# Output tiles in fp16, cast to fp32 by the software DMA queue, with more buffers and right halves stored between whole rows

## The chip, the cores and the metric

The kernel runs on one core of one Trainium2 chip. The metric is device time in microseconds (us), the median of several executions. All runs in this document are with one core in use. Ratios and their 95% intervals are over fast runs of the same rounds; they are not quite the ratio of the medians quoted beside them. The span of a profile is about 2 us shorter than the device time of the same execution (182.8 and 184.6 us for the kernel before). In the profile's lines PE is the matrix engine, DVE the vector engine, ACT the scalar engine, POOL is GpSimd and SP the sync engine. "DMA engine" means one of the core's 16 DMA engines. A run of bytes is a contiguous piece that a transfer reads or writes, 1 KB or 2 KB here.

## The reference, cut to what matters

Windowed attention (8 batches, 8 heads, 576 positions, head size 64) feeds a soft mixture of experts. Only the end of the second part matters here:

```python
# x: [4608, 512], the attention output; phi: [512, 32]; w1: [8, 512, 1024]; w2: [8, 1024, 512]
...
for e in range(E):
    h = np.maximum(slot_input[e] @ w1[e], 0.0)
    slot_out[e] = h @ w2[e]
slot_out = slot_out.reshape(n_slots, D)          # [32, 512]
c = softmax(logits, axis=1)                      # [4608, 32]; cut
return (c @ slot_out).astype(np.float32)         # [4608, 512] fp32: 9.44 MB
```

All inputs and the output are fp32 in HBM. A row of the output holds 512 numbers: 2 KB in fp32.

## The kernel before: the parts that the argument touches

The loads are issued by GpSimd on the software DMA queue and cast from fp32 to fp16 on the way. The weights `w2` of experts 6 and 7 are loaded by column halves, so that the left half of the output can start while the weights of the right half still arrive. The output then goes out in 26 transfers: 8 left halves of 256 rows each, 10 whole pairs of 128-row blocks, 8 right halves. In the code `fp` is the product in PSUM and `rrow` holds the reciprocals of the softmax row sums.

```python
out_pool = tc.alloc_tile_pool(name="outp", bufs=NSPLIT // 2)      # NSPLIT = 16, NH = 256
...
def combine(half, pair):                       # 256 rows, half of the columns: runs of 1 KB
    ...                                        # two matmuls into PSUM tile fp
    ot = out_pool.tile([128, 2, NH], FP32, name=f"ot{half}_{pair}", tag="ot")
    if pair % 2 == 0:
        ...                                    # ACT: two activations with scale=rrow
    else:
        nc.vector.tensor_tensor(out=ot, in0=fp, in1=rrow[...], op=ALU.mult)
    nc.sync.dma_start(out=out[r0 : r0 + 256, NH * half : NH * half + NH].rearrange("(k p) n -> p k n", k=2), in_=ot)

def combine_full(pair):                        # 256 whole rows: runs of 2 KB
    ot = out_pool.tile([128, 2, DMODEL], FP32, name=f"of_{pair}", tag="of", bufs=5)
    for k in range(2):
        ...                                    # one matmul; ACT scales k = 0, DVE k = 1
    nc.sync.dma_start(out=out[r0 : r0 + 256, :].rearrange("(k p) n -> p k n", k=2), in_=ot)

slot_out(0, ORDER[:6]); slot_out(1, ORDER[:6]); slot_out(0, HALVED)
for pair in range(NSPLIT // 2):
    combine(0, pair)                           # left halves
    ...                                        # expert 6 of the right half after pair 5
slot_out(1, HALVED[1:])
for pair in range(NSPLIT // 2, NFIN // 2):
    combine_full(pair)                         # whole rows
for pair in range(NSPLIT // 2):
    combine(1, pair)                           # right halves
```

The softmax here doesn't subtract the row's maximum and nothing guards it: scores larger than these inputs give would overflow.

## Time and profile before

| | before |
|---|---|
| median of 3 runs | 184.9 us (184.83 to 185.29) |
| busy share of PE, DVE, ACT, GpSimd | 78%, 57%, 49%, 34% |
| last weight landed | 156.95 us |
| last output landed | 181.66 us |
| end of the span | 182.8 us |

The profile's page of the kernel before: the DMA row gives the busy tenths of the 16 DMA engines in 40 slices of the span, the row below it the GB/s that they wrote (a cast load counts with its fp16 side), and the queue rows packets, MB and share.

```profile
span 182.8 us, 5535 instructions
...
DMA  5999999999999999999999999999999999999996
GB/s 88 195 198 211 203 208 206 211 209 204 213 207 204 213 208 204 213 208 204 213 208 204 212 212 213 216 214 214 215 214 216 196 196 183 328 376 387 380 351 219
...
q0 software_dynamic: 24640, 31.10, 97.6%
q1 hardware_dynamic: 7360, 9.56, 14.9%
...
out_dram<-of SPq DMA_DIRECT2D x10, 512.0 KB, 5.5
...
out_dram<-ot SPq DMA_DIRECT2D x16, 256.0 KB, 3.9
```

The DMA engines are full in all but the first and the last slice. Up to slice 34 (about 155 us) they load; about 210 GB/s of fp16 are 420 GB/s of fp32 read. In the last six slices they store. The outputs are nearly all of q1's 9.56 MB.

The end of the chain that ended last, of the kernel before: start, length, engine or DMA, what.

```profile
146.53 10.42 DMA w<-in_moe_w_dram
156.99 0.32 PE so L681 x4
157.33 0.38 ACT so_sb L689
...
162.03 10.45 DMA out_dram<-of x2
172.47 0.68 DVE ot L713
```

It waits for the last weight, and then for transfers of the output. Engines compute only in the gaps.

The waits of the kernel before from 145 us on: who waited for what, us in total, times, longest.

```profile
ACT of L732 <- DMA out_dram<-of: 5.1, 5, 2.7
DVE of L736 <- DMA out_dram<-of: 3.6, 4, 2.0
```

With five buffers for whole-row tiles, ACT and DVE stand still for 8.7 us (the sum of both) until stores free a buffer.

The stretches view of the kernel before, one for whole rows (2 KB runs) and one for right halves (1 KB runs): busy us of PE, weight loads, DVE, ACT and GpSimd, then the granted clock, the DMA share and GB/s.

```profile
165.00:171.00 6.00, 4.07 (x16) 1.92 (x15) 3.85 (x6) 4.10 (x8) 0.00 (x0) 0.64 1.04 384
176.00:180.00 4.00, 0.00 (x0) 0.00 (x0) 0.00 (x0) 0.00 (x0) 0.00 (x0) 0.50 1.03 345
```

Divided over 16 engines, 384 GB/s is one 2 KB run per 85.3 ns, and 345 GB/s one 1 KB run per 47.5 ns. A straight line through these two rates has 37.8 ns for each KB and a fixed part of 9.7 ns for each run. The share of 1.03 says that packets hardly overlap.

### The profile page before, as it was taken

The numbers are of one execution on the slowest core, as the hardware profiler recorded it, in microseconds if no ns is written. First come the engines' busy times: TensorE is split into PE (matmuls) and PEld (weight loads), VectorE is DVE, ScalarE is ACT, GpSimd is POOL, SyncE is SP. The second block draws the span as 40 slices with busy tenths as digits, with TensorE's granted clock in tenths as the row PEclk, the third lists the DMA queues.
The fourth block names the chain that finished last, engine by engine and source line by source line (L and its number), as shares of the span: only waits on it lengthen the run. The fifth ranks groups of instructions, "written<-read, shape, count | busy, mean of one in ns | idle before, by whom it ended". The sixth has DMA issues, their size and how long they took to land.

```text
span 182.8 us, 5535 instructions
## 1 busy us (share of the span) xinstructions
PE 142.9 (78%) x2448; PEld 85.6 (47%) x2448; DVE 104.2 (57%) x225; ACT 90.1 (49%) x161; POOL 62.6 (34%) x86
## 2 busy tenths in 40 slices
PE   0467989999999999999999999998694087746600
PEld 0134556557557557557557557573532063312300
DVE  2585797958767867867867865360502004555700
ACT  2044267667666766766766766734002005644800
POOL 7643644652651751751822935311110110000000
PEclk9999999999999999999999999985569667897555
DMA  5999999999999999999999999999999999999996
GB/s 88 195 198 211 203 208 206 211 209 204 213 207 204 213 208 204 213 208 204 213 208 204 212 212 213 216 214 214 215 214 216 196 196 183 328 376 387 380 351 219
DMA packets 32024, 41.01 MB, mean 224 GB/s; under 512 B 2144, under 2 KB 19680, under 8 KB 32000
## 3 DMA queue, kind: packets, MB, share of 16 engines
q0 software_dynamic: 24640, 31.10, 97.6%
q1 hardware_dynamic: 7360, 9.56, 14.9%
q8 instruction: 19, 0.31, 0.6%
q14 instruction: 5, 0.04, 0.1%
HBM read 62.18 MB, written 9.44 MB: 392 GB/s over the span
## 4 chain that ended last, share of the span: by engine, by line
DMA 48%; PE 27%; issue 7%; ACT 6%; POOL 4%; DVE 3%; SPq 0%; POOLq 0%
DMA w<-in_moe_w_dram 34%; DMA raw<-in_q_dram 8%; DMA out_dram<-of 6%; PE lg L413 5%; PE o_p L344 5%; PE sa L287 4%; ACT p L298 4%; PE sa L276 3%; PE sb L276 3%; ACT of L732 2%; PE u L455 2%; PE rd L394 1%; PE vb L188 1%; PE va L188 1%; POOL w L220 1%
## 5 line engine op out<-in xcount | busy, mean ns | idle before, releaser
L298 ACT ACTIVATE p<-sa 128x960 f16<-128x960 f32 (+2 forms) x24 | 21.4, 890 | 30.2 <-PE sb L287 29.5
L344 PEld LDWEIGHTS <-p 128*128 128x128 f16 (+2 forms) x544 | 19.5, 98 | 12.6 <-issue 8.6
L241 DVE STREAM_TRANSPOSE qk<-raw 128x576 uint32<-128x576 uint32 x16 | 20.0, 1250 | 6.8 <-DMA raw<-in_q_dram 5.9
L250 DVE STREAM_TRANSPOSE qk<-raw 128x320 uint32<-128x320 uint32 (+1 forms) x32 | 21.5, 678 | 0.3
L298 ACT ACTIVATE p<-sb 128x960 f16<-128x960 f32 (+2 forms) x24 | 21.2, 885 | 0.0
L276 PE MATMUL sa<-masks,ident 128*128 128x480 f16 (+2 forms) x48 | 13.8, 372 | 6.6 <-DMA ident<-ident_d 4.9
L413 PE MATMUL lg<-xTd,phi 128*128 128x288 f16 x32 | 18.3, 659 | 0.0
L287 PE MATMUL sa<-qk 32*128 32x160 f16 (+4 forms) x416 | 15.7, 212 | 2.4 <-DVE qk L241 2.4
L287 PEld LDWEIGHTS <-qk 32*128 32x128 f16 x832 | 11.9, 96 | 11.8 <-issue 8.2
L276 PEld LDWEIGHTS <-ident 128*128 128x128 f16 x96 | 8.9, 102 | 17.4 <-issue 8.7
L216 POOL COPY v<-v 32x1024 f16<-32x1024 f16 x8 | 8.3, 1034 | 25.4 <-DVE v L209 22.9
L344 PE MATMUL o_p<-v,p 128*128 128x65 f16 (+1 forms) x288 | 16.4, 201 | 0.7 <-ACT v L197 0.7
L287 PE MATMUL sb<-qk 32*128 32x160 f16 (+4 forms) x416 | 15.7, 212 | 0.0
L232 POOL DMA_DIRECT2D w<-in_moe_w_dram x8 | 5.9, 742 | 27.2 <-DMA w<-in_moe_w_dram 22.8
L366 DVE TENSOR_TENSOR xp<-o_p,rc_p 128x448 f16<-128x448 f32 (+1 forms) x24 | 14.5, 602 | 0.8
L366 DVE TENSOR_TENSOR xd<-o_d,rc_d 128x448 f16<-128x448 f32 (+1 forms) x24 | 14.5, 602 | 0.8
L713 DVE TENSOR_TENSOR ot<-f,rrow 128x512 f32<-128x512 f32 x8 | 5.5, 690 | 15.8 <-PE f L697 15.6
L276 PE MATMUL sb<-masks,ident 128*128 128x480 f16 (+2 forms) x48 | 14.0, 372 | 0.4 <-issue 0.2
L681 PE MATMUL so<-w,hTm 128*32 128x256 f16 x128 | 7.0, 354 | 8.5 <-DMA w<-in_moe_w_dram 7.7
L220 POOL DMA_DIRECT2D w<-in_moe_w_dram x16 | 11.4, 715 | 5.5 <-DMA raw<-in_k_dram 2.1
L188 PE MATMUL va<-vs,orders 32*128 32x256 f16 (+1 forms) x96 | 12.1, 289 | 1.0 <-ACT p L298 1.0
L417 ACT ACTIVATE ET<-lg 128x288 f16<-128x288 f32 x16 | 6.6, 410 | 12.0 <-PE lg L413 11.8
(84 smaller groups left out, 251.7 us busy)
## 6 DMA issues: line engine op xcount, KB each, us to landing
w<-in_moe_w_dram POOLq DMA_DIRECT2D x16, 512.0 KB, 16.6
w<-in_moe_w_dram POOLq DMA_DIRECT2D x6, 1024.0 KB, 28.1
out_dram<-of SPq DMA_DIRECT2D x10, 512.0 KB, 5.5
vs<-in_v_dram POOLq DMA_DIRECT2D x8, 512.0 KB, 13.1
out_dram<-ot SPq DMA_DIRECT2D x16, 256.0 KB, 3.9
raw<-in_q_dram POOLq DMA_DIRECT2D x7, 576.0 KB, 15.1
raw<-in_k_dram POOLq DMA_DIRECT2D x7, 576.0 KB, 15.4
w<-in_moe_w_dram POOLq DMA_DIRECT2D x8, 256.0 KB, 23.3
```

Of the source, the lines that this page charges most:

```text
L188: nc.tensor.matmul(o.rearrange("p (h d) -> p h d", h=4), l, st[:, 0:4, D * r : D * r + D], start=(r == 0), stop=(r == DIL - 1), skip_group ...
L216: nc.gpsimd.tensor_copy(out=vL[b % NV][0:32, :, :, 0:D], in_=vD[b % NV][96:128, :, :, 0:D])
L220: nc.gpsimd.dma_start(out=w1t[e][:, 2 * i : 2 * i + 2, :], in_=src[:, 2 * i : 2 * i + 2, :])
L241: nc.vector.transpose(out=dst, in_=src)
L250: nc.vector.transpose(out=o, in_=i)
L276: nc.tensor.matmul(sps[h // 2][:, h % 2, 0:n], ident, bias[g], start=True, stop=False, skip_group_check=True,)
L287: nc.tensor.matmul(sps[h // 2][:, h % 2, c0 : c0 + w], kt_[32 * h : 32 * h + 32, k0 : k0 + 128, tt], qt_[32 * h : 32 * h + 32, q0 : q0 + w ...
L298: nc.scalar.activation(out=pt, in_=sps[ab][:, :, 0:n], func=AF.Exp, scale=SCALE)
L344: nc.tensor.matmul(o[p0 : p0 + np_, n, :], l, rr, start=(k == 0), stop=(k == len(jobs) - 1), skip_group_check=True,)
L366: nc.vector.tensor_tensor(out=x.rearrange("p t (h d) -> p (t h) d", h=4)[0:nq, u0:u1, :], in0=o[0:nq, 0:n, 0:D], in1=rc[0:nq, 0:n, None].b ...
L413: nc.tensor.matmul(lp, phi4[:, kc].rearrange("p c s -> p (c s)"), rhs, start=(kc == 0), stop=(kc == 3))
L681: nc.tensor.matmul(so[half][32 * a : 32 * a + 32, :], hTm[2 * g + c // 4][:, c % 4, 32 * j : 32 * j + 32], w2t[e][:, c, NH * half : NH * h ...
```

## The change

The intent: half the bytes read from SBUF per output, room for 24 buffers for the 26 output tiles in place of 13 (the last two whole-row tiles reuse buffers), no waits for buffers, and a smoother mix of small and large stores. A cast in flight is done by the software queue only, as the Trainium skill has it ("DMA: Bandwidth & Descriptors", section "SWDGE vs HWDGE vs iDMA"), so the stores move from the sync engine's queue to GpSimd's.

```diff
-    out_pool = tc.alloc_tile_pool(name="outp", bufs=NSPLIT // 2)
+    out_pool = tc.alloc_tile_pool(name="outp", bufs=1)
...
-        ot = out_pool.tile([128, 2, NH], FP32, name=f"ot{half}_{pair}", tag="ot")
+        ot = out_pool.tile([128, 2, NH], FP16, name=f"ot{half}_{pair}", tag=f"ot{half}", bufs=NSPLIT // 2)
...
-        nc.sync.dma_start(
+        nc.gpsimd.dma_start(                      # in combine and in combine_full
...
-        ot = out_pool.tile([128, 2, DMODEL], FP32, name=f"of_{pair}", tag="of", bufs=5)
+        ot = out_pool.tile([128, 2, DMODEL], FP16, name=f"of_{pair}", tag="of", bufs=8)
...
             combine_full(pair)
-        for pair in range(NSPLIT // 2):
-            combine(1, pair)
+            if pair >= NFIN // 2 - NSPLIT // 2:
+                combine(1, pair - (NFIN // 2 - NSPLIT // 2))
```

More of the change, by code (lines that the diff above doesn't have):

```diff
@@ L742, in combine_full @@
                 )
-        nc.sync.dma_start(
+        nc.gpsimd.dma_start(
             out=out[r0 : r0 + 256, :].rearrange("(k p) n -> p k n", k=2), in_=ot
```

## The prediction

> **What bounds the kernel now.** The DMA engines, all the way. The page's DMA row is at 9 in nearly every slice; PE is busy 78%, DVE and ACT about half. Up to about 155 us the software queue loads and casts fp32 inputs and weights; the chain of waits is mostly DMA w<-in_moe_w_dram, ending at 156.99 when the last weight lands, then ACT so_sb, then out_dram. From 154 to 181.7 us the 9.44 MB of output drain. In the stretches view the whole-row stores (2 KB runs) move 383-387 GB/s and the half-row stores (1 KB runs) 332-351 GB/s, without pause; the idle end is 1.1 us.
>
> **Time by packets.** In the trace's packet records a plain 1 KB store takes 46-48 ns, a 2 KB one 84-88 ns, one after another on each engine: about 8 + 38 ns per KB. A cast load of 1 KB of fp32 (512 B written) takes 60 ns but overlaps: 383 start per us on 16 engines, one each 41.8 ns. So per engine the stores are 16 x 16 x 46.7 ns + 10 x 16 x 85 ns = 25.6 us. The engines are not level: the last weight lands on the first at 152.97 us and on the last at 156.95. The late ones set the end.
>
> **What changes.**
> 1. fp16 output tiles. SBUF reads halve, but HBM still gets 9.44 MB of fp32, same runs. ACT (0.69 us per 128x512, 0.42 per 128x256) and DVE (0.75; 0.69 for the 128x512 product) read fp32 PSUM as before: no time saved there.
> 2. Own buffers. The 8.7 us in which ACT and DVE wait for out_dram<-of vanish. They are off the critical path: the queue is full meanwhile. Worth about 0.
> 3. Issue moves from SP (0.66 and 1.2 us each) to POOL, idle by then: 26 x 0.7 us (its 256-run loads take 0.70) = 18 us within a 25 us drain. Each issue also waits for the transfer eight earlier on that queue (order of instructions); eight outputs are about 7 us of work, so it stays fed.
> 4. The Trainium skill, "DMA: Bandwidth & Descriptors", section "SWDGE vs HWDGE vs iDMA", says a cast needs the software queue, and that both kinds feed different queues of the same engines. So weights and outputs now stand in one queue: late engines can't slip outputs between weights (some 0.8 us now).
> 5. Right halves between whole rows: same bytes; 0.
>
> **Sum.** If cast stores cost what plain ones do: late engines start at 156.95, +25.6, +1.4 = 184.0 span, 1.2 worse. If they overlap like cast loads (estimate 41.8 and 79.5 ns): 23.4 us of drain, span 181.8, 1.0 better. I lean to the second. I expect no halving, as the written side stays fp32, though no trace here separates read limit from write limit: if reads alone limit, POOL issue, about 18 us, binds.
>
> Predicted 183.9 us (before 184.9), 8 in 10 between 179.0 and 187.5. Faster by over 2%: 0.2; within 2%: 0.64; slower by over 2%: 0.16.
>
> **What would show it.** Output packets on the software queue: about 60 ns (1 KB) and 98 ns (2 KB), overlapping, GB/s near 390 for halves and 405 for rows after 158 us; no ACT or DVE wait for out_dram; POOL issues of about 0.7 us; the last weight landing unchanged at 156-157 us.
>
> **What would make it wrong.** Upcasting slower or faster than its fp32 bytes; POOL issuing well over 0.9 us per output; waits for the eighth-earlier transfer starving the queue at the switch from loads to stores.

## The result, and the profile after

The changed kernel took 183.96 us (183.67 to 184.2, 4 runs) against 184.87 us (4 runs): ratio 0.9947 [0.9925, 0.9969], within 2%. A second measurement with more rounds gave 0.9952 [0.9932, 0.9972]. So it is a small gain of 0.9 us, clear of noise.

The page of the changed kernel:

```profile
span 181.9 us, 5521 instructions
...
GB/s 74 191 207 214 200 212 202 212 210 202 213 210 205 209 211 202 214 209 205 210 210 203 211 212 212 218 211 217 215 213 215 200 196 169 334 403 410 406 409 140
...
q0 software_dynamic: 31712, 40.54, 119.8%
...
L719 POOL DMA_DIRECT2D out_dram<-ot x16 | 11.3, 710 | 7.0 <-ACT ot L709 7.0
...
out_dram<-of POOLq DMA_DIRECT2D x10, 512.0 KB, 6.3
...
out_dram<-ot POOLq DMA_DIRECT2D x16, 256.0 KB, 4.7
```

All output now stands in q0. GpSimd issues a store in 0.71 us. The drain, the time in which the stores go out, runs at 403 to 410 GB/s per slice where it ran at 351 to 387.

The waits of the changed kernel from 145 us on have one line left that ends with a store, and it is GpSimd's own issue:

```profile
POOL out_dram L743 <- DMA out_dram<-of: 0.5, 1, 0.5
```

The stretches view of the changed kernel; its third row is the mix of whole rows and right halves:

```profile
154.00:156.00 2.00, 2.00 (x16) 0.84 (x14) 1.39 (x2) 1.31 (x5) 2.00 (x3) 0.50 1.14 192
156.00:158.00 2.00, 1.53 (x13) 0.63 (x12) 0.69 (x1) 1.28 (x4) 2.00 (x4) 0.69 1.89 376
165.00:171.00 6.00, 1.85 (x9) 0.59 (x7) 2.96 (x5) 2.23 (x5) 4.55 (x8) 0.99 1.65 407
```

The DMA share is now 1.65 to 1.89: packets of one engine overlap. The trace's packet records give 80 ns for a 1 KB packet and 115 ns for a 2 KB one. They were 47 and 86 ns before, so each packet takes longer and yet more bytes move.

Where did the time go? The landing records of the trace hold one landing per DMA engine and transfer:

| us | before | after |
|---|---|---|
| last weight, first and last engine | 152.97, 156.95 | 153.17, 156.54 |
| last output, first and last engine | 181.40, 181.66 | 179.11, 180.47 |
| from last weight to last output | 24.71 | 23.93 |
| from last output to the end of the span | 1.16 | 1.42 |

The stores end 0.8 us sooner after the last weight. The weight itself came 0.4 us sooner in this execution, and the end cost 0.3 us more. Together that is the 0.9 us of the spans. These shares are of one execution each: a second profile of the changed kernel (e4 below) has 156.50 us for the last weight and 23.55 us from it to the last output, so they are good to some 0.4 us. The last weight came between 156.4 and 157.3 us in the profiles of all kernels here.

### The profile page after: what moved, and what is told of

Its sections match the earlier page's. It is cut to its first block, busy times and chain, and to the rows that moved or that the text cites. A ratio compares the mean times of both kernels' runs of the same rounds, so it can differ in the third digit from the quotient of the medians.

```text
span 181.9 us, 5521 instructions
## 1 busy us (share of the span) xinstructions
PE 144.2 (79%) x2448; PEld 85.8 (47%) x2448; DVE 104.1 (57%) x225; ACT 90.2 (50%) x161; POOL 80.9 (44%) x112
## 3 DMA queue, kind: packets, MB, share of 16 engines
HBM read 62.18 MB, written 9.44 MB: 394 GB/s over the span
## 4 chain that ended last, share of the span: by engine, by line
DMA 38%; PE 33%; POOL 8%; ACT 7%; issue 7%; DVE 3%; POOLq 1%
DMA w<-in_moe_w_dram 27%; DMA raw<-in_q_dram 6%; PE lg L413 5%; DMA vs<-in_v_dram 5%; ACT p L298 5%; PE sa L287 4%; PE o_p L344 4%; PE sb L276 4%; PE sa L276 3%; PE f L697 2%; PE rd L394 2%; PE u L455 2%; POOL out_dram L719 1%; ACT of L732 1%; PE vb L188 1%
## 5 line engine op out<-in xcount | busy, mean ns | idle before, releaser
L287 PEld LDWEIGHTS <-qk 32*128 32x128 f16 x832 | 12.6, 100 | 14.9 <-issue 9.6
L287 PE MATMUL sa<-qk 32*128 32x160 f16 (+4 forms) x416 | 16.2, 217 | 4.1 <-DVE qk L241 4.1
L276 PE MATMUL sa<-masks,ident 128*128 128x480 f16 (+2 forms) x48 | 15.0, 401 | 4.4 <-DMA ident<-ident_d 3.1
L276 PEld LDWEIGHTS <-ident 128*128 128x128 f16 x96 | 9.5, 109 | 15.8 <-issue 8.7
L287 PE MATMUL sb<-qk 32*128 32x160 f16 (+4 forms) x416 | 16.3, 217 | 0.0
L276 PE MATMUL sb<-masks,ident 128*128 128x480 f16 (+2 forms) x48 | 15.2, 403 | 0.5 <-ACT p L298 0.5
L719 POOL DMA_DIRECT2D out_dram<-ot x16 | 11.3, 710 | 7.0 <-ACT ot L709 7.0
L713 DVE TENSOR_TENSOR ot<-f,rrow 128x512 f16<-128x512 f32 x8 | 5.5, 688 | 11.5 <-PE f L697 11.4
```

The lines of the kernel that those rows point to most:

```text
L276: nc.tensor.matmul(sps[h // 2][:, h % 2, 0:n], ident, bias[g], start=True, stop=False, skip_group_check=True,)
L287: nc.tensor.matmul(sps[h // 2][:, h % 2, c0 : c0 + w], kt_[32 * h : 32 * h + 32, k0 : k0 + 128, tt], qt_[32 * h : 32 * h + 32, q0 : q0 + w ...
L719: nc.gpsimd.dma_start(out=out[r0 : r0 + 256, NH * half : NH * half + NH].rearrange("(k p) n -> p k n", k=2), in_=ot,)
```

## The experiments

Every experiment was timed in rounds with the kernel before, and every kernel except one (e7) gave the right result. Three theories stood at first: C, a cast store overlaps in the engine as a cast load does (the prediction's); Q, the software queue does this for any store; B, the gain comes from own buffers and order.

### e1: the software queue alone

```diff
-        nc.sync.dma_start(      # before, both places
+        nc.gpsimd.dma_start(    # fp32 tiles, 8 and 5 buffers, order as before
```

> The kernel before with its outputs issued by the software queue, still fp32, buffers and order unchanged. Theory C (the cast makes stores overlap in an engine): packets stay at about 46 and 85 ns, one after another, the drain per engine stays near 25.6 us, ratio to before 1.000 to 1.008 (one queue for weights and outputs costs up to 1.2 us). Rival Q (the software queue alone makes stores overlap, whatever the type): packets of 60 to 80 ns (1 KB) that overlap, over 400 GB/s written in the drain, ratio 0.993 to 0.997. Rival B (own buffers and order gave the gain): 0.999 to 1.001.

Measured: 187.62 us against 184.76, ratio 1.0162 [1.0136, 1.0187], outside every range expected. Its stretches (whole rows, right halves):

```profile
165.00:171.00 6.00, 3.69 (x12) 1.37 (x11) 3.27 (x5) 3.10 (x6) 2.86 (x4) 0.59 1.01 370
178.00:182.00 4.00, 0.00 (x0) 0.00 (x0) 0.00 (x0) 0.00 (x0) 0.72 (x1) 0.50 0.96 313
```

Q falls: nothing overlaps (0.96 to 1.01), and the stores are slower than on the sync queue, 370 and 313 GB/s against 384 and 345. The loss of 2.9 us is also more than twice the 1.2 us that theory C had allowed. The packet records show why the packets look different: the queue joined the runs into 4096-byte packets (median 175 ns in the whole rows). That agrees with the section "SWDGE vs HWDGE vs iDMA" of the skill's page, which calls 4096 B or less the preferred packet; the cast stores of the changed kernel, though, stayed at 1024 and 2048 B.

### e2: the cast alone

```diff
-        ot = out_pool.tile([128, 2, NH], FP32, ...)       # e1
+        ot = out_pool.tile([128, 2, NH], FP16, ...)       # the same for the whole-row tile
```

> fp16 tiles and cast by the software queue alone; buffer counts (8 and 5) and order as before. Theory C: the whole gain, ratio 0.992 to 0.997, packets of 80 and 115 ns as in the changed kernel, ACT and DVE still waiting for out_dram. Q: the same ratio. B: no gain, 0.999 to 1.002.

Measured: 183.77 us against 184.76, ratio 0.9952 [0.9931, 0.9973], the same as the whole change in the same rounds. Its stretches and its waits:

```profile
165.00:171.00 6.00, 4.62 (x13) 1.72 (x13) 3.97 (x6) 3.72 (x7) 2.83 (x5) 0.50 1.47 414
176.00:178.00 2.00, 0.00 (x0) 0.00 (x0) 0.00 (x0) 0.00 (x0) 2.00 (x4) 0.50 1.95 393
```

```profile
ACT of L732 <- DMA out_dram<-of: 4.8, 4, 3.2
DVE of L736 <- DMA out_dram<-of: 4.0, 4, 2.6
```

ACT and DVE still wait 8.8 us for buffers, and it costs nothing. With halved reads the same queue moves 414 GB/s and 393 GB/s. From e1 to e2 only the type of the tiles changed, and 3.85 us were won (187.62 to 183.77).

### e3: own buffers and order alone

fp32 tiles on the sync queue. The 26 tiles in fp32 are 72 KB per partition, and whole rows and right halves lie in the space of the first-layer weights, which are done with by then.

```diff
+    pairs4 = [w1_pool.tile([128, 2, 2, DMODEL], FP32, name=f"of4_{i}", tag=f"w1_{i}") for i in range(5)]
+    halves4 = [w1_pool.tile([128, 4, 2, NH], FP32, name=f"ot4_{i}", tag=f"w1_{5 + i}") for i in range(2)]
...                                     # stores by nc.sync, order as in the changed kernel
-        ot = out_pool.tile([128, 2, DMODEL], FP16, name=f"of_{pair}", tag="of", bufs=8)
+        ot = pairs4[i // 2][:, i % 2]  # i = pair - NSPLIT // 2
```

> Own buffers for every output and right halves between whole rows alone: fp32 tiles, sync queue; the extra buffers lie in the space of the first-layer weights, which are done with. Theories C and Q: no wait of ACT or DVE for out_dram is left, and yet ratio 0.998 to 1.002, drain at 340 to 387 GB/s. B: 0.993 to 0.997.

Measured: 184.76 us against 184.76, ratio 0.9997 [0.9972, 1.0022]. The waits view has no wait of an engine for a store left. The mixed stretch runs at 368 GB/s, between the 345 and 384 of the kernel before:

```profile
165.00:171.00 6.00, 2.27 (x11) 0.86 (x9) 3.35 (x5) 2.79 (x6) 0.00 (x0) 0.87 1.03 368
```

B falls. 8.7 us of waiting were taken away and nothing was gained.

### e4: the changed kernel again

No edit.

> The changed kernel once more in the same rounds, for a tighter interval: all theories 0.993 to 0.997 (0.9947 was measured).

Measured: 183.83 us, ratio 0.9952 [0.9932, 0.9972].

### e6: a cast with 4-byte reads

Apart from the size of e1's loss, C had passed so far. But e2 mixes two things: the transfer is a cast, and its source is half as wide. The output seen as float32r makes a cast of a store that is 4 bytes wide on both sides.

```diff
-            out=out[r0 : r0 + 256, :].rearrange("(k p) n -> p k n", k=2), in_=ot              # e1
+            out=out[r0 : r0 + 256, :].rearrange("(k p) n -> p k n", k=2).bitcast(mybir.dt.float32r), in_=ot
...                                     # and the same for the halves
```

> As e1_pool_fp32 (software queue, fp32 tiles, buffers and order as before), with the output seen as float32r, which the software queue should treat as a cast although both sides are 4 bytes wide. What the cast brings was still mixed with reading 2 bytes instead of 4. Theory C1 (the kind of transfer that a cast makes is what overlaps): packets of 60 to 80 ns per 1 KB that overlap, no merging into 4 KB packets, ratio 0.993 to 0.998. Theory C2 (the smaller read is what counts): slower stores again, ratio 1.005 to 1.02.

Measured: 187.83 us against 184.53, ratio 1.0175 [1.0149, 1.0201]. Its stretches:

```profile
165.00:171.00 6.00, 3.77 (x10) 1.29 (x10) 3.00 (x4) 2.75 (x4) 2.29 (x4) 0.50 1.22 369
179.00:182.00 3.00, 0.00 (x0) 0.00 (x0) 0.00 (x0) 0.00 (x0) 0.71 (x1) 0.50 1.36 322
```

The packets did change kind: 1024 and 2048 B again in place of 4096, 65 to 67 and 105 ns each, and they overlap (1.22 to 1.36). Yet the rate is that of e1. So overlap as such is not what saves time, and C in the prediction's form falls too. What counts is the narrower source: e6 and e2 differ only in the width of the tiles (and in the float32r view).

### e7: a source of one byte

The changed kernel with fp8 tiles. The result is wrong (relative error 1.0).

```diff
-        ot = out_pool.tile([128, 2, DMODEL], FP16, ...)
+        ot = out_pool.tile([128, 2, DMODEL], mybir.dt.float8e4, ...)   # and the halves; saturate=False where written
```

> The changed kernel with fp8 output tiles, cast to fp32 by the software queue: the result is wrong in its digits on purpose. Reads per output fall to a quarter of fp32, writes stay. Theory W (with a narrow source the written side alone sets the pace, and halving was enough): packets again about 80 and 115 ns, one 1 KB run each 41 ns, 2 KB each 79 ns, ratio to before 0.993 to 0.998, as with fp16. Theory R (the bytes read still count): over 430 GB/s written, ratio below 0.992.

Measured: 183.59 us against 184.56, ratio 0.9944 [0.9919, 0.9969]. The mixed stretch runs as with fp16 (407 GB/s):

```profile
165.00:171.00 6.00, 1.60 (x8) 0.57 (x6) 2.72 (x5) 2.00 (x4) 4.79 (x8) 0.83 1.75 408
```

Quartering the read brings no more than halving it (packets 87 and 122 ns, still overlapping). Below 4 bytes the source's width no longer counts. The pace is then set by something that both kernels share: the bytes written, the number of elements, or the number of packets. e7 does not separate these; v1 below makes the whole-row packets twice as long and gains little (412 GB/s for 407).

The rates of the runs, worked out as for the kernel before (16 engines times the run's bytes, over the stretch's GB/s; the drain is 256 runs of 1 KB and 160 of 2 KB per engine):

| stores | 1 KB run | 2 KB run | per KB | fixed part | drain per engine | last weight to last output |
|---|---|---|---|---|---|---|
| before: sync queue, fp32 | 47.5 ns | 85.3 ns | 37.8 | 9.7 | 25.8 us | 24.71 us |
| e1: software queue, fp32 | 52.3 | 88.6 | 36.3 | 16.0 | 27.6 | 27.34 |
| e6: software queue, 4-byte cast | 50.9 | 88.8 | 37.9 | 13.0 | 27.2 | 27.69 |
| e2: software queue, from fp16 | 41.7 | 79.1 | 37.4 | 4.3 | 23.3 | 24.01 |

A KB costs about the same in all four. By this reckoning the kinds of store differ in the fixed part of a run. The fixed part is twice one rate less the other, so it moves with the stretch: with whole rows at 163 to 172 us, and halves at 176 to 181 us before, 177.5 to 181.5 in e1, 178.5 to 182.5 in e6 and 175 to 179 in e2, it is about 9, 12, 12 and 5 ns. e1 and e6 are therefore not told apart, and only the order holds: the fp16 source lowest, then the sync queue, then the 4-byte sources on the software queue. In e1 the runs were joined into larger packets, so its figure is not one for a packet.

### h1: left halves stay on the sync queue

```diff
-        ot = out_pool.tile([128, 2, NH], FP16, ...)
+        ot = out_pool.tile([128, 2, NH], (FP32, FP16)[half], ...)
-        nc.gpsimd.dma_start(
+        (nc.sync, nc.gpsimd)[half].dma_start(     # whole rows: gpsimd, 6 buffers
```

> The changed kernel, but the eight left half tiles stay fp32 and go by the sync queue, as before; whole rows and right halves are cast by the software queue. It tests the prediction's step 4, that in one queue the late engines can't slip outputs between weights. If that costs 0.8 us: these eight outputs cost 0.7 us more on each engine as plain stores and gain up to 0.8 us, so 0.993 to 0.997 of before. If slipping is worth nothing: 0.997 to 1.000. If both kinds of stores overlap with each other as loads and stores do: below 0.993.

Measured: 185.17 us against 184.53, ratio 1.003 [1.0008, 1.0052], above every figure expected. Two things are seen. The first whole row was issued at 160.2 us and the queue ran low:

```profile
160.00:162.00 2.00, 2.00 (x9) 0.91 (x8) 1.46 (x3) 1.71 (x4) 1.58 (x3) 0.63 0.98 316
```

And GpSimd's drain (the DRAIN instruction of that engine at the end of the program, after which the last semaphores follow) ended 1.97 us after the last landing (0.66 us in the changed kernel). The drain accounts for most of what h1 lost to the changed kernel (1.5 us between the two spans): from the last weight to the last output h1 took 23.77 us, like the changed kernel (23.93, and 23.55 in e4's profile), but from there to the end of the span 2.76 us against 1.42. So nothing was gained where slipping should have shown, but the low queue may have hidden it, and what slipping outputs between weights is worth stays open.

### v1, v2 and v4: longer runs, fewer halves

If the fixed part of a run is what counts, fewer and longer runs should gain. v1 puts rows 2p and 2p + 1 of a whole-row pair on partition p, so that a run is 4 KB:

```diff
+    def rows_of(cols, k):
+        return cols.rearrange("c (p k) -> c k p", k=2)[:, k, :]
...                                     # row sums of these blocks with rows_of, too
-            nc.tensor.matmul(fp, ET[:, 128 * blk : 128 * blk + 128], so_sb, start=True, stop=True)
+            nc.tensor.matmul(fp, rows_of(ET[:, r0 : r0 + 256], k), so_sb, start=True, stop=True)
...
-            out=out[r0 : r0 + 256, :].rearrange("(k p) n -> p k n", k=2), in_=ot
+            out=out[r0 : r0 + 256, :].rearrange("(p k) n -> p k n", k=2), in_=ot
```

> The changed kernel with rows 2p and 2p + 1 of a whole-row pair on partition p, so that a store's runs are 4 KB in place of 2 KB; the matmul takes every second column of ET as weights. With a fixed part of about 4 ns per run (1 KB every 41 ns, 2 KB every 79.5 ns), 80 runs fewer per engine save 0.3 us: ratio to before 0.991 to 0.996, 4 KB packets of about 190 ns, one each 155 ns per engine. If the strided weight load slowed the PE, nothing would show while the drain is fed.

v2 is v1 with `NSPLIT = 12` and 12 whole-row buffers:

> v1_runs_4k with 6 instead of 8 row pairs stored in halves. 128 runs fewer per engine than the changed kernel: 0.5 us, ratio 0.990 to 0.995; if the six left halves don't cover the time until the first whole rows are ready, the queue runs dry around 160 us and it is no better than v1.

v4 is v1 with `NSPLIT = 14` and 11 whole-row buffers:

> v1_runs_4k with 7 row pairs in halves, between v1 (8) and v2 (6). v2 lost in two ways: the queue ran low around 160 to 162 us (303 GB/s) and GpSimd's drain ended 2.2 us after the last landing. If 7 left halves cover the gap and the drain ends within 0.7 us: ratio 0.991 to 0.995. If the gap is the reason and grows steadily from 8 to 6: 0.996 to 1.000. If the late drain is there too: 1.000 to 1.006.

| | time | before, same rounds | ratio | GpSimd's drain ends after the last landing |
|---|---|---|---|---|
| v1, 8 halves | 183.37 us | 184.53 | 0.9940 [0.9918, 0.9963] | 0.45 us |
| v4, 7 halves | 183.42 | 184.56 | 0.9934 [0.9913, 0.9956] | 0.37 |
| v2, 6 halves | 185.55 | 184.53 | 1.0053 [1.0034, 1.0072] | 2.21 |

v1 moves 412 GB/s in the mixed stretch (407 in the changed kernel). v1 and v4 have the best ratios of all correct kernels here. Against the changed kernel's 0.9952 the difference is 0.1 to 0.2%, within the intervals, so it is not settled that they beat it, or that longer runs pay. Both lie in the ranges expected; v2 does not.

v2 lost. The two lines below are v2's and v4's stretch in which the left halves are out and the whole rows begin:

```profile
160.00:162.00 2.00, 2.00 (x6) 0.60 (x5) 1.71 (x3) 1.42 (x4) 1.28 (x4) 0.50 0.93 303
```

```profile
160.00:162.00 2.00, 1.99 (x6) 0.62 (x5) 1.79 (x3) 1.59 (x4) 1.12 (x2) 0.57 1.06 260
```

v4 ran lower there and was still fast. v2's last output landed at 180.27 us and v1's at 179.77, 0.5 us apart, while their spans are 183.2 and 181.0. From the last landing to the end v2 takes 2.96 us and v1 1.21. Most of v2's loss is therefore after the last landing, in GpSimd's late drain.

### v3 and d1: the last right halves on the sync queue

v3 is v1 with its last two right halves in fp32 by `nc.sync`; d1 is v2 with its last three, and with 10 whole-row buffers in place of 12.

```diff
-        nc.gpsimd.dma_start(
+        (nc.sync if (half, pair) >= (1, NSPLIT // 2 - 2) else nc.gpsimd).dma_start(     # d1: - 3
```

> v1_runs_4k with its last two right halves in fp32 by the sync queue. In the changed kernel GpSimd's own drain ends 0.66 us after the last landing (before, nothing waits for it); if it can end while the sync queue's two outputs still land, 0.2 to 0.6 us are saved, less 0.15 us for the two plain stores: ratio to before 0.990 to 0.994. If two queues at once slow each other: 0.994 to 0.998.

> v2_runs_4k_split12 with its last three right halves in fp32 by the sync queue, so that GpSimd's drain starts from an earlier last transfer. If GpSimd's late drain was what cost v2 its end (2.2 us after the last landing): the drain now ends before or soon after the last landing, and the ratio falls from 1.005 to 0.992 to 0.999. If v2's loss was the gap at 160 us: it stays at 1.003 to 1.007.

Measured: v3 183.78 us against 184.56, ratio 0.9946 [0.9923, 0.9969]: no gain over v1. It lies in the range for two queues that slow each other, but the interval covers the other range too. d1 185.5 us, ratio 1.0051 [1.0026, 1.0076]: no better than v2. That would make the gap at 160 us the reason; but d1's profile has the late drain still, 2.09 us after the last landing. The edit did not do what it was meant to, in v3 and d1 alike: the sync queue's stores overtook, and the last output to land was still one of GpSimd's (v3: 180.90 us against 177.20 for the last of the sync queue; d1: 181.11 against 180.95). So d1 did not tell the two apart, and only v4 and the arithmetic above speak. Why the drain is late in v2, h1 and d1, and in none of the other kernels that store by this queue, stays open.

## Why the prediction was right or wrong

The predicted time was 183.9 us and the predicted span 181.8 us in the case that it leaned to; 183.96 and 181.9 came. The mechanism was only half right, and that the number fits so well is partly luck: two terms were off in opposite directions, the cost of the queue (step 4) and the worth of the cast (the sum). In the sum's own terms, 156.95 + 23.4 + 1.4 was predicted and 156.54 + 23.93 + 1.42 came: the last weight 0.4 us earlier, the stores after it 0.5 us longer.

- **Step 1, compute gains nothing.** Right: DVE's half-row product takes 688 ns in place of 690.
- **Step 2, own buffers are worth about 0.** Right: e3, ratio 0.9997; e2 keeps the waits and has the whole gain.
- **Step 3, GpSimd's issue keeps up.** Right: 0.71 us an issue, and one wait of 0.5 us for an earlier transfer.
- **Step 4, one queue costs some 0.8 us (1.2 us in the sum, with the longer end).** Mis-sized. Moving fp32 stores to the software queue cost 2.9 us (e1). The prediction took plain stores to cost the same 46.7 and 85 ns on either queue. On the software queue they took 52.3 and 88.6 ns, 1.8 us more in the drain per engine. Also the late engines no longer caught up: the last output's landings were 0.26 us apart before and 1.87 us in e1. One queue alone need not do that: in v2 and v4, whose stores all go by it too, they were 0.33 and 0.29 us apart. What slipping outputs between weights was worth stays open (h1).
- **Step 5, the order is worth 0.** Right, by e3.
- **The sum: "If they overlap like cast loads".** The run costs were right, 41.7 and 79.1 ns measured against 41.8 and 79.5, and so was the drain, 23.3 us against 23.4. The reason was wrong, so that the rates of the loads carried over was luck as far as these runs show. e6's stores are casts and overlap, at the pace of e1. It is the source of half the width that counts, and it is worth 3.85 us (e1 to e2), where the prediction had 2.2 us (25.6 less 23.4), because it counted from the sync queue's cost.
- **No halving.** Right: e7 reads a quarter and moves 408 GB/s like fp16's 407. That it is the written side that limits is likely but not shown; the numbers of elements and of packets stay the same too.
- **Packet times.** Predicted 60 and 98 ns, measured 80 and 115. The rates predicted, near 390 and 405 GB/s, were met (393 and 414 in e2). Here a packet's duration said little about its cost once packets overlapped.

So the expected gain of halved reads is there, 3.85 us, and three quarters of it pay for the queue that a cast needs, 2.9 us. The rest, about 1 us, is the result.

## What to carry to other kernels

The cast brought the software queue with it, and here that queue alone cost 2.9 us while the narrower source gave back 3.85 us: price the two separately, by building each alone. Where DMA is the bottleneck, as here, waits of compute engines for output buffers can be a mere symptom: removing 8.7 us of them moved nothing. Compare DMA rates per run and stretch, not packet durations, since overlapping packets take longer and can still move more.

## What the Trainium skill lacked or had wrong

- "DMA: Bandwidth & Descriptors", section "Issuing engine by pattern", says that HWDGE (here the sync queue) is generally faster than SWDGE (the software queue); the page has first-byte latencies for the two, but no rates that compare their stores on trn2. The same 9.44 MB of fp32 stores made the kernel 2.9 us slower by the software queue, at 370 and 313 GB/s against 384 and 345 (2 KB and 1 KB runs).
- The same page, section "Why small descriptors are slow (HBM only)", gives a fixed part per packet, of about 3 cycles. It lacks that the fixed part of a store depends on the queue and on the source's width: about 9.5 ns for a run (sync, fp32), 12 to 16 ns (software, 4-byte source), 4 to 5 ns (software, fp16 to fp32), all worked out from two stretches a kernel. Why the width matters is not shown by these runs.
- The same page, section "SWDGE vs HWDGE vs iDMA", says which queue casts, but not what a cast costs. Measured: an fp16 or fp8 source cast to fp32 stores at 407 to 408 GB/s written in the same mix; a 4-byte source seen as a cast is no faster than a plain store (369 against 370 GB/s).
- The same section prefers packets up to 4096 B. Plain software-queue stores were joined to 4096 B; cast ones went out as single runs of 1024 or 2048 B (in v1, with runs of 4 KB, of 4096 B).
- No page has GpSimd's drain at the end of a program whose last stores it issued: it ended 0.4 to 0.7 us after the last landing in most of these kernels, and 2.0 to 2.2 us after it in three.
